# A statically planned attention and two-layer expert kernel: new engine choices for three kinds of operations, and its instruction order searched anew

## The chip, the core and the metric

The program runs on one core of a Trainium2 chip, in one launch. The metric is the device time of that launch in microseconds (us). TensorE (PE in the profile) multiplies matrices, and its weight loads stand beside it as PEld. VectorE (DVE), ScalarE (ACT) and GpSimd (POOL) do elementwise work, and SyncE (SP) issues every transfer.

## The reference, cut to what is computed

```python
# attention: 4 batches, 8 heads, 576 positions, head size 64
scores = q @ k.T / sqrt(64)
x      = log1p(abs(i - j)) / log1p(max(i, 1))        # one number per (i, j)
bias   = relu(x * w1 + b1) @ w2                      # 32 inner units -> 8 heads
attn   = softmax(scores + bias) @ v                  # 2304 tokens x 512
# first expert layer pair, 512 -> 2048 -> 512
g1     = s * relu(attn @ w_in) ** 2 + b
y1     = g1 @ w_out
# second expert layer pair, 512 -> 2048 -> 512
h      = y1 @ w2_in
y2     = (h - tanh(h)) @ w2_out
```

The four large weights come as 64-bit floats, so the kernel also turns them into 32-bit values on VectorE (three instructions for each half of a weight pair, lines 1253, 1256 and 1259). Products are made of two 16-bit parts: each fp32 operand is split into a high and a low half, and three products are added. The second layer pair uses a seven-product block scheme (in_product and out_product) in place of eight.

## The kernel before, in words

The program is one list of tasks. Each task has the engines that could run it with a cost for each (`sc.add({DVE: 0.16, POOL: 0.3}, mx_add, ...)`), the tasks that it depends on, and a priority. Before a single instruction is issued, `Schedule.forward` plays this list through a model in Python: engines become free, transfers land after a planned delay, buffers of a ring come free, and among the tasks that can start first the one with the smallest priority number is taken. The sequence in which the model starts tasks is the order in which each engine's instructions are written into its queue. At run time each engine goes through its own queue in that order and waits on semaphores where an input is late.

Five tables steer the model. `COST` corrects the cost of a kind of task on an engine. `XFER` gives a factor on the length of a transfer and a delay after it. `PORT` says which VectorE tasks count as users of what VectorE and GpSimd share. `ENGINE` limits single tasks to named engines; a key such as `u7.hi` holds for all tasks of that name in its tag. `SHIFT` adds a number to the priority of every key, and it is the result of a search. `QG` is the number of bias row groups whose inner layer may run on GpSimd.

The work in the order of time:

- Weights and bias. The first layer pair's weights are loaded, converted and split. The bias has 36 row groups Q (tags bias0 for Q 0 to 7, up to bias4 for Q 32 to 35); each has four inner-layer instructions (`hid`, lines 727 and 730, one for each quarter of the 32 units' rows), matrix products (`mm`, line 761), and a copy out (`out`).
- Attention. There are 144 units: 128 rows of scores of one head. For each: `qk` (line 1041), bias addition and row minimum of the negated scores on VectorE (`ttr`, line 1073), an offset added to that row value (`mx_add`, line 1081, 128x1 elements), the exponential on ScalarE (`ex`, line 1087, which reads the offset value as its bias), high and low halves (`hi`, `lo_a`, `lo_b`; lines 1097 to 1104), a transposing transfer (`tr`, line 1119), and the product with v (`pv`, line 1132). The tags are u0 to u9 for units 0 to 39 (four units each), u12 for 40 to 47 and u13 to u18 for 16 units each. Four units make a group, which is scaled, split and transposed again (tags x0 to x18).
- First layer pair. Nine blocks of 256 tokens (tags f0 to f8). A block has eight pairs of hidden slices: products into PSUM (`ph`, line 1573), ReLU from PSUM (`relu`, line 1586), square, high and low halves; then 16 product tasks into `po` (line 1645) and the copy out (`out`, lines 1659 and 1664).
- The point called `turn`. When all attention is done, its memory is given to the second layer pair, whose weights are then loaded, converted, split and added up (tags L0, L1, P00 to P11; lines 1253 to 1259, 615 to 618 and 1852).
- Second layer pair. 18 sets (tags I0 to I17 for the first product, J0 to J17 for the second), with seven products each. Here the order of the products on TensorE is fixed in the code, one after the other (`last_pe`). Four products of a set leave PSUM through `copy` on ScalarE (line 2057); the others are read by VectorE. High halves of the result (`split`, key I.lambda) can run on ScalarE or VectorE.

Of the kernel before, what the change touches and what calls it, by code (L numbers as in the profile page):

```python
# [26 lines left out]
SHARE0, QP, QA, SCU, QG = 21, 8, 16, 12, 7  # L27
# [3 lines left out]
AHEAD = 6.97  # L31
# [4 lines left out]
    "u.ttr@dve": 0.84944, "f.hi@dve": 1.152216, "u.hi@dve": 0.87312, "s.in_done@dve": 1.1143, "scan.add@dve":  # L36
    0.8125, "f.lambda@dve": 1.174, "s.out_done@dve": 1.662, "u.lo@pool": 0.9991, "f.lo@pool": 0.782085,
    "bias.lambda@pool": 1.0466, "u.qk@pe": 0.885, "u.pv@pe": 0.97, "u.tr@sp": 1.04, "x.lambda@sp": 1.083,
    "q.fn@sp": 1.36, "J.c@dve": 1.2701, "J.fn@dve": 1.12, "L.lambda@dve": 1.0069, "L.square@act": 0.919,
    "P.wsum@dve": 1.0042, "X.scales@dve": 0.7943, "X.sums@dve": 1.21, "X.xsum@dve": 1.1245, "bias.lambda@dve":  # L40
    1.0453, "bias.out@dve": 1.179, "f.norm@dve": 1.2446, "f.out@dve": 1.0696, "f.scales@dve": 0.4404,
    "k.hi@dve": 1.1296, "k.lambda@dve": 1.047, "q.hi@dve": 1.1098, "s.lambda@dve": 1.0224, "scan.lambda@dve":
    0.857, "v.hi@dve": 1.738, "v.lambda@dve": 1.0251, "w.lambda@dve": 0.993, ".begin@dve": 0.784, ".lambda@dve":
    1.116, "L.scales@dve": 0.961, "L.sums@dve": 0.868, "X.lambda@act": 1.021, "X.lambda@dve": 1.023,
    "q.lambda@dve": 1.026, "w.scale_out@dve": 0.859, "u.lo@act": 0.97, "u.lo_a@act": 0.97, "u.lo_b@act": 0.97,
    "u.lo@dve": 0.97, "u.lo_a@dve": 0.97, "u.lo_b@dve": 0.97, "u.lo_a@pool": 0.97, "u.lo_b@pool": 0.97,
    "f.lo@act": 0.85, "f.lo@dve": 0.85, "f.hi@act": 1.04, "f.hi@pool": 1.04, "u.hi@pool": 0.8, "u.ex@dve": 0.8,
    "u.ex@pool": 0.8, "u.ttr@act": 0.8, "u.ttr@pool": 0.8,
}
XFER = {  # L50
    "bias.fn": (0.79893, 1.75), "f.fn": (1.5147, 1.23), "k.fn": (1.07019, 1.73), "q.fn": (1.05633, 1.81),
    "scan.fn": (0.80982, 2.01), "u.fn": (1.21869, 1.21), "u.tr": (1.0197, 2.23), "v.fn": (0.97218, 2.27),
    "w.fn": (0.91872, 2.03), "x.fn": (1.188, 1.54), "x.lambda": (0.81873, 1.51), "L.fn": (0.87714, 2.6), "J.fn":
    (0.33264, 1.52), "X.fn": (1.54341, 1.41), "o.fn": (0.8514, 0.99), ".fn": (0.78903, 1.4),
}
# [3 lines left out]
    "x.recip": 0.0,  # L59
# [5 lines left out]
    "dve", "u12.lo_a": "pool", "u12.lo_b": "pool", "u13.lo_a": "pool", "u13.lo_b": "pool", "u17.lo_b": "pool",  # L65
# [201 lines left out]
class Schedule:  # L267
# [13 lines left out]
    def add(self, opts, fn, deps=(), prio=0.0, takes=(), uses=(), after=(), share=None):  # L281
# [6 lines left out]
        for e, c in opts.items():  # L288
            if len(opts) == 1 or only is None or e in only:
                if isinstance(c, tuple):  # L290
                    k, d = XFER.get(kind, (0.99, 1.79))
                    t.opts[e] = (c[0] * 0.95 * COST.get(kind + "@" + e, 1.0), c[1] * k, d)
                else:
                    t.opts[e] = c * COST.get(kind + "@" + e, 1.0)
# [2032 lines left out]
```

## Time and profile before

| what | value |
|---|---|
| median of three runs | 1053.27 us (1051.8 to 1054.85) |
| the profiled execution | 1057.96 us |
| its span, first to last instruction | 1056.2 us |
| TensorE busy | 964.1 us, 91% of the span |
| VectorE busy | 881.6 us, 83% |
| ScalarE busy | 667.5 us, 63% |
| GpSimd busy | 250.1 us, 24% |
| mean granted TensorE clock | 0.954 |

The profile is of one execution. It is 4.69 us above the median of the runs, and 1.76 us of it lie outside the span. A share of the whole span says little in this kernel, since the limits differ from stage to stage; the stretches below are therefore read one by one. [...]

### The profile page before, as it was taken

To read this page: it belongs to the slowest core of one execution; us is meant where nothing else is said; L and a number is where in the kernel's file an instruction comes from. 1 tells how busy PE (TensorE), PEld (TensorE's weight loads), DVE (VectorE), ACT (ScalarE), POOL (GpSimd) and SP (SyncE) were. 2 spreads that over 40 slices of the span, in tenths; PEclk is the share of its full clock that TensorE was granted. 3 is DMA by queue.
4 is the path that set the end of the run, shared out by engine and by line. 5 is a ranking of instruction groups with operands and counts; after the bars stand their busy time and mean duration, and the time that the engine had idled before them with its cause. 6 is when DMAs were issued, how large, how long until landed. Compare 5 with 4: busy or idle time off the path is not lost.

```text
span 1056.2 us, 32450 instructions
## 1 busy us (share of the span) xinstructions
PE 964.1 (91%) x13486; PEld 833.2 (79%) x13486; DVE 881.6 (83%) x1918; ACT 667.5 (63%) x1307; POOL 250.1 (24%) x319
## 2 busy tenths in 40 slices
PE   5676678999988999999997999988999999999998
PEld 3233356778767788788886888878999999999998
DVE  6999899876568677786774889999999999999885
ACT  4797659749767565776853687766554555464452
POOL 6146437247542334455511000000000000000000
PEclk9767679899999999999999999998999999999999
DMA  9969995899999879999896904410001100100000
GB/s 341 398 227 216 311 236 119 184 200 252 245 197 230 168 179 176 201 188 207 171 180 104 397 21 138 148 36 12 32 23 32 52 23 22 42 22 23 22 22 22
DMA packets 261444, 153.66 MB, mean 145 GB/s; under 512 B 197680, under 2 KB 229552, under 8 KB 261296
## 3 DMA queue, kind: packets, MB, share of 16 engines
q1 hardware_dynamic: 261296, 151.59, 59.1%
q8 instruction: 105, 1.72, 0.7%
q14 instruction: 43, 0.35, 0.1%
HBM read 84.03 MB, written 20.33 MB: 99 GB/s over the span
## 4 chain that ended last, share of the span: by engine, by line
PE 43%; DVE 9%; ACT 3%; DMA 2%; issue 2%; POOL 1%; SPq 0%; DVEq 0%; ACTq 0%; POOLq 0%
PE acc L2166 14%; PE pa L2038 9%; PE pb L2038 7%; PE po L1645 5%; PE ph L1573 4%; PE po L2166 2%; DMA et<-hl 2%; DVE w2big L1852 2%; DVE w2big L618 1%; PE sp L1041 1%; DVE w1big L618 1%; ACT e L1087 1%; POOL hl L1104 1%; PE xp L1132 1%; DVE hr L1603 1%
## 5 line engine op out<-in xcount | busy, mean ns | idle before, releaser
L1645 PE MATMUL po<-hr,w1big 128*128 128x256 f16 x1728 | 202.9, 274 | 3.6 <-ACT x L1664 2.7
L1104 POOL TENSOR_TENSOR hl<-e,hl 128x64 f16<-128x64 f32 (+1 forms) x200 | 160.2, 818 | 184.9 <-ACT hl L1099 107.2
L1573 PEld LDWEIGHTS <-w1big 128*128 128x128 f16 x1728 | 166.9, 99 | 31.5 <-issue 10.6
L1645 PEld LDWEIGHTS <-w1big 128*128 128x128 f16 x1728 | 165.5, 98 | 26.5 <-issue 7.1
L2038 PEld LDWEIGHTS <-w2big 128*128 128x128 f16 x3024 | 175.2, 99 | 2.2 <-issue 2.1
L2166 PEld LDWEIGHTS <-w1big 128*128 128x128 f16 x3024 | 172.8, 98 | 0.0
L1087 ACT ACTIVATE e<-sp,mx 128x576 f32<-128x576 f32 x144 | 105.6, 735 | 70.3 <-POOL mx L1081 34.3
L1073 DVE CUSTOM_DVE_ANT_0 sp<-sp,bi 128x576 f32<-128x576 f32 x144 | 107.0, 772 | 20.2 <-PE sp L1041 16.2
L1573 PE MATMUL ph<-xt_own,w1big 128*128 128x256 f16 x960 | 113.1, 274 | 3.0 <-ACT r L1586 2.2
L1041 PE MATMUL sp<-ks,qs 64*128 64x288 f16 (+1 forms) x960 | 84.2, 296 | 25.8 <-ACT e L1087 24.8
L1573 PE MATMUL ph<-w1big 128*128 128x256 f16 x768 | 91.2, 276 | 3.3 <-ACT r L1586 2.6
L1041 PEld LDWEIGHTS <-qs 64*128 64x128 f16 (+1 forms) x960 | 48.7, 99 | 53.0 <-issue 42.2
L1132 PEld LDWEIGHTS <-et 128*128 128x128 f16 (+1 forms) x1440 | 54.7, 104 | 41.2 <-issue 21.5
L1132 PE MATMUL xp<-vp,et 128*128 128x64 f16 (+1 forms) x1440 | 65.4, 199 | 19.1 <-DMA et<-hl 11.7
L2166 PE MATMUL acc<-hr,w1big 128*128 128x128 f16 x1296 | 79.9, 219 | 0.0
L1099 ACT ACTIVATE hl<-e 128x576 f16<-128x576 f32 x96 | 64.7, 678 | 23.1 <-DMA et<-hl 20.2
L2166 PE MATMUL acc<-w2big,w1big 128*128 128x128 f16 x1296 | 79.0, 219 | 0.0
L1104 DVE TENSOR_TENSOR hl<-e,hl 128x512 f16<-128x512 f32 (+1 forms) x88 | 48.8, 572 | 15.9 <-ACT hl L1099 13.0
L2038 PE MATMUL pa<-w1big,w2big 128*128 128x128 f16 x960 | 59.9, 219 | 1.7 <-ACT w2big L2057 0.9
L1586 ACT ACTIVATE r<-ph 128x512 f32<-128x512 f32 x72 | 42.3, 590 | 25.8 <-PE ph L1573 21.3
L1591 ACT ACTIVATE r<-r,sq 128x512 f32<-128x512 f32 x72 | 51.2, 718 | 0.9
L2074 ACT ACTIVATE w1big<-w1big 128x512 f32<-128x512 f32 x34 | 21.3, 630 | 45.6 <-DVE w1big L2064 33.4
(229 smaller groups left out, 1757.7 us busy)
## 6 DMA issues: line engine op xcount, KB each, us to landing
bi<-btd SPq DMA_DIRECT2D x64, 288.0 KB, 4.1
w1big<-in_wout SPq DMA_DIRECT2D x12, 1024.0 KB, 6.0
btd<-et SPq DMA_DIRECT2D x36, 295.5 KB, 3.7
w1big<-in_win SPq DMA_DIRECT2D x8, 1024.0 KB, 9.7
w2big<-in_win SPq DMA_DIRECT2D x8, 1024.0 KB, 13.1
x2d<-x SPq DMA_DIRECT2D x36, 128.0 KB, 3.1
w1big<-x2d SPq DMA_DIRECT2D x36, 128.0 KB, 2.3
outT<-xt_own SPq DMA_DIRECT2D x18, 256.0 KB, 2.2
```

The source lines that it names most:

```text
L1041: nc.tensor.matmul(out=out, lhsT=qs.tile[64 * h:64 * h + 64, sq, p * r:p * r + r], rhs=ks.tile[64 * h:64 * h + 64, sk, half * HS:(half + 1 ...
L1073: nc.vector.tensor_tensor_reduce(out=st, in0=st, in1=bi.tile.rearrange("p (a b) -> p a b", a=2), scale=-1.0 / KAP, scalar=3.0e38, op0=ALU. ...
L1087: nc.scalar.activation(out=put(e, row_tile("e")).rearrange("p (a b) -> p a b", a=2), in_=sp.tile[:, :, 0:HS], func=AF.Exp, scale=-1.0, bia ...
L1099: nc.scalar.activation(out=h[:, 0:S], in_=e.tile, func=AF.Copy)
L1104: eng_of(eng).tensor_tensor(out=hl.tile[:, o:o + m], in0=e.tile[:, c:c + m], in1=hl.tile[:, c:c + m], op=ALU.subtract)
L1132: nc.tensor.matmul(out=xp[r0:r0 + r, o:o + 64], lhsT=et.tile[:, n, r0:r0 + r], rhs=vp.tile[:, 0, n % 5, 64 * h:64 * h + 64], start=n == 0, ...
L1573: nc.tensor.matmul(out=ph.tile[:, fi, :], lhsT=win_ap(1, sw, m, f), rhs=xa(sx, m), start=m == 0 and j == 0, stop=m == KM - 1 and j == 2,)
L1586: nc.scalar.activation(out=r.tile, in_=ph.tile, func=AF.Relu)
L1591: nc.scalar.activation(out=r.tile, in_=r.tile, func=AF.Square, scale=sq[:, fp // 4:fp // 4 + 1])
L1645: nc.tensor.matmul(out=po.tile[:, :NB1], lhsT=wout_ap(1, sw, f, c), rhs=rhl[f // 8][:, f % 8, sr, :], start=f == 0 and j == 0, stop=f == K ...
L2038: nc.tensor.matmul(out=bank.tile[:, f * HT:(f + 1) * HT], lhsT=w[:, sw, m, f * 128:(f + 1) * 128], rhs=xs[:, sx, m], start=p in (1, 2, 5) ...
L2166: nc.tensor.matmul(out=bank.tile[:, o + c * HT:o + (c + 1) * HT], lhsT=w[:, sw, f, c * 128:(c + 1) * 128], rhs=g[:, sx, f], start=new and ...
```

## The change

Three operations get a further engine: the offset of the row value may run on ScalarE (`mx_add`, an ACTIVATE with the function Copy and a constant bias), the ReLU of the first layer pair may run on VectorE (a maximum with 0), and the copies of the products of the second pair may run on VectorE. `QG` goes from 7 to 36, so that the inner layer of every bias row group may run on GpSimd, at a planned cost of 5.0e-3 us per column in place of 4.2e-3. The planner's tables are corrected: eight costs of VectorE go up, every transfer's delay goes down by 0.36 us except those of bias rows and of the two transposing transfers, which go up by 0.44 to 0.45 us; `AHEAD` goes from 6.97 to 6.93. GpSimd tasks with a share of 0 no longer wait in the model for VectorE. `ENGINE` has 138 entries in place of 124; of those, 81 are as before. In `SHIFT`, no number is as before (the two sets of numbers have a correlation of 0.59).

In the diff below the entries of the tables are grouped, and only those that the text speaks of are kept.

```diff
-SHARE0, QP, QA, SCU, QG = 21, 8, 16, 12, 7
+SHARE0, QP, QA, SCU, QG = 21, 8, 16, 12, 36
-AHEAD = 6.97
+AHEAD = 6.93
 COST = {
-    "u.hi@dve": 0.87312, "scan.add@dve": 0.8125, "f.lambda@dve": 1.174, "f.scales@dve": 0.4404,
-    "k.hi@dve": 1.1296, "q.hi@dve": 1.1098, "scan.lambda@dve": 0.857, "u.lo_a@dve": 0.97,
-    "bias.lambda@pool": 1.0466,
+    "u.hi@dve": 0.95168, "scan.add@dve": 1.0563, "f.lambda@dve": 1.3736, "f.scales@dve": 0.5065,
+    "k.hi@dve": 1.412, "q.hi@dve": 1.3318, "scan.lambda@dve": 0.9598, "u.lo_a@dve": 1.358,
...
 XFER = {
-    "f.fn": (1.5147, 1.23), "u.fn": (1.21869, 1.21), "u.tr": (1.0197, 2.23), "x.lambda": (0.81873, 1.51),
+    "f.fn": (1.5147, 0.87), "u.fn": (1.21869, 1.65), "u.tr": (1.0197, 2.68), "x.lambda": (0.81873, 1.95),
...
 PORT = {
-    "x.recip": 0.0,
+    "x.recip": 0.0, "x.eps": 0.0,
 ENGINE = {
+    "f0.relu": "act", "f1.relu": "act", "f2.relu": "act", "f3.relu": "act", "f4.relu": "act", "f8.relu": "act",
+    "u18.mx_add": "act+pool", "u15.mx_add": "dve+pool", "u16.mx_add": "dve+pool", "u17.mx_add": "dve+pool",
+    "u9.mx_add": "dve+pool", "u7.mx_add": "pool",
-    "u3.mx_add": "pool",
+    "u3.mx_add": "dve",
+    "bias1.lambda": "act+dve", "bias3.lambda": "act+dve",
-    "u7.hi": "act", "u7.lo_a": "dve", "x2.lo": "dve", "x7.lo": "dve", "x7.hi": "dve", "x17.hi": "dve",
+    "u7.hi": "dve", "u7.lo_a": "pool", "x2.lo": "pool", "x7.lo": "pool", "x7.hi": "act", "x17.hi": "act",
+    "u2.lo_a": "pool", "I7.lambda": "act", "I16.lambda": "act", "I10.lambda": "dve", "I15.lambda": "dve",
-    "I5.lambda": "dve", "I6.lambda": "act",
+    "I5.lambda": "act", "I6.lambda": "dve",
...
+        if only is not None and not any(e in only for e in opts):
+            only = None
...
-                    elif eng == "pool" and t.opts[eng] < self.LONG:
+                    elif eng == "pool" and t.share > 0.0 and t.opts[eng] < self.LONG:
...
             if Q < QG:
-                opts[POOL] = 4.2e-3 * n
+                opts[POOL] = 5.0e-3 * n
...
         def mx_add(eng):
             m = mx["m"]
-            eng_of(eng).tensor_scalar(out=m, in0=m, scalar1=LN_E, scalar2=None, op0=ALU.add)
-        t_mx = sc.add({DVE: 0.16, POOL: 0.3}, mx_add, [t_ttr[u]], d + 1.5)
+            if eng == ACT:
+                nc.scalar.activation(out=m, in_=m, func=AF.Copy, bias=LN_E)
+            else:
+                eng_of(eng).tensor_scalar(out=m, in0=m, scalar1=LN_E, scalar2=None, op0=ALU.add)
+        t_mx = sc.add({DVE: 0.16, POOL: 0.31, ACT: 0.2}, mx_add, [t_ttr[u]], d + 1.5)
...
-            def relu(_, fp=fp, ph=ph, r=r):
+            def relu(e, fp=fp, ph=ph, r=r):
                 put(r, r_p.tile([128, 2, NB1], F32, tag="r", name="r")[:, :, :w])
-                nc.scalar.activation(out=r.tile, in_=ph.tile, func=AF.Relu)
-            tr = sc.add({ACT: 0.21 + 0.8e-3 * 2 * w}, relu, tp + [t_bs], ready - 400, [r], [ph])
+                if e == DVE:
+                    nc.vector.tensor_scalar(out=r.tile, in0=ph.tile, scalar1=0.0, scalar2=None, op0=ALU.max)
+                else:
+                    nc.scalar.activation(out=r.tile, in_=ph.tile, func=AF.Relu)
+            tr = sc.add(
+                {ACT: 0.21 + 0.8e-3 * 2 * w, DVE: 0.12 + 1.05e-3 * 2 * w}, relu, tp + [t_bs], ready - 400, [r], [ph],
+                share=0.0,
+            )
...
         def copy(n, bank):
             i = st[n] = inst("E")
             st["t", n] = sc.add(
-                {ACT: 0.68}, lambda _: nc.scalar.activation(out=home(i), in_=bank.tile, func=AF.Copy, scale=ich),
-                [t] + (first_use["E"] if k < 2 else []), pr - 300, [i], [bank],
+                {ACT: 0.68, DVE: 0.66}, lambda e: copy_scale(home(i), bank.tile, ich, e),
+                [t] + (first_use["E"] if k < 2 else []), pr - 300, [i], [bank], share=0.0,
             )
```

## Rows read from the trace of the kernel before

**Rows 1.** The page: busy us, share of the span and instructions of each engine.
```profile
PE 964.1 (91%) x13486; PEld 833.2 (79%) x13486; DVE 881.6 (83%) x1918; ACT 667.5 (63%) x1307; POOL 250.1 (24%) x319
```

**Rows 2.** Busy time by stretch: stretch, length, each engine, PE clock, DMA share, GB/s.
```profile
0.00:26.00 26.00, 14.12 (x145) 8.32 (x149) 16.27 (x35) 12.62 (x22) 15.66 (x12) 0.95 0.92 340
26.00:106.00 80.00, 53.09 (x459) 25.39 (x451) 78.71 (x155) 66.45 (x134) 33.63 (x27) 0.72 0.87 281
106.00:158.00 52.00, 34.64 (x387) 22.64 (x385) 46.95 (x103) 32.95 (x73) 21.98 (x26) 0.74 1.09 276
158.00:561.00 403.00, 387.15 (x5170) 318.20 (x5166) 300.23 (x801) 283.33 (x633) 177.18 (x253) 0.99 0.96 192
561.00:616.00 55.00, 49.87 (x529) 43.51 (x530) 35.94 (x61) 25.84 (x62) 1.64 (x3) 0.97 0.69 230
616.00:721.00 105.00, 94.17 (x942) 84.18 (x939) 100.20 (x158) 80.66 (x137) 0.00 (x0) 0.99 0.26 82
721.00:845.00 124.00, 123.90 (x2169) 123.91 (x2169) 120.63 (x252) 66.36 (x101) 0.00 (x0) 0.98 0.11 32
845.00:1003.00 158.00, 158.00 (x2828) 158.00 (x2825) 145.03 (x295) 79.49 (x119) 0.00 (x0) 1.00 0.08 26
```

**Rows 3.** TensorE's waits from 158 to 721 us: total, times, longest.
```profile
PE sp L1041 <- ACT e L1087: 8.5, 13, 2.3
PE xp L1132 <- DMA et<-hl: 5.6, 6, 2.5
PE ph L1573 <- ACT r L1586: 4.8, 6, 2.0
PE psum L695 <- DVE w2big L2064: 3.9, 1, 3.9
PE po L1645 <- ACT x L1664: 2.7, 2, 1.6
PE pa L2038 <- ACT w2big L2057: 0.9, 1, 0.9
```

**Rows 4.** The chain that ended last, one piece of it: start, length, what.
```profile
677.92 4.44 DMA w1big<-x2d
```

**Rows 5.** Transfers by line: size or none for transposes, median us to landing.
```profile
et<-hl SPq DMA_TRANSPOSE x144, 4.0
```

**Rows 6.** Waits of all engines from 528 to 561 us.
```profile
ACT e L1087 <- POOL mx L1081: 6.0, 4, 2.3
```

**Rows 7.** Instruction groups of the whole span: busy us, mean ns, idle before.
```profile
L1586 ACT ACTIVATE r<-ph 128x512 f32<-128x512 f32 x72 | 42.3, 590 | 25.8 <-PE ph L1573 21.3 <-DVE hr L1603 4.3
...
L1087 ACT ACTIVATION_READ_ACCUMULATOR e<-sp,mx 128x1 f32 x144 | 28.1, 195 | 0.0
...
L1081 POOL TENSOR_SCALAR mx<-mx 128x1 f32<-128x1 f32 x61 | 18.2, 299 | 42.3 <-DVE mx L1073 36.7 <-DVE nm L1554 2.3 <-DVE s L899 0.5
...
L2064 DVE SCALAR_TENSOR_TENSOR w1big<-pb,cols,w1big 128x512 f32<-128x512 f32 x18 | 13.4, 747 | 8.6 <-PE pb L2038 8.6
...
L1081 DVE TENSOR_SCALAR mx<-mx 128x1 f32<-128x1 f32 x83 | 12.0, 149 | 1.0
```

**Rows 8.** Line 2057, the 72 copies: what ScalarE sat idle for before them.
```profile
  PE pa L2038: 41.8, 35
  PE pb L2038: 9.6, 7
```

**Rows 9.** Groups by shape: inner layer of the bias, weight conversion at two times.
```profile
L730 POOL TENSOR_SCALAR hr<-u_sb,cst_sb 128x512 f32<-128x512 f32 x2 | 4.7, 2342 | 0.2 <-DVE qkc L824 0.2
...
L1259 DVE SCALAR_TENSOR_TENSOR w1big<-w1big 128x1024 uint32<-128x1024 uint32 x16 | 21.5, 1348 | 0.1
...
L1259 DVE SCALAR_TENSOR_TENSOR w2big<-w2big 128x1024 uint32<-128x1024 uint32 x8 | 9.5, 1219 | 0.0
```

**Rows 10.** ScalarE in order of time, one inner-layer instruction of Q = 7: start, length.
```profile
32.66 0.67 ACT L727 ACTIVATE xt_own<-u_sb,cst_sb 128x464 f32<-128x464 f32 x1
```

**Rows 11.** The row values' reads: ns (min/median/max), first and last start.
```profile
L1073 DVE DVE_READ_ACCUMULATOR2_ANT mx<- x144: 132/141/145, 60.6 to 559.4; 128x1 f32 x144
```

More of the change, by code (lines that the diff above doesn't have):

```diff
@@ L35 @@
     "w.square@act": 1.07, "k.hi@act": 1.15, "s.lambda@act": 1.09, "q.hi@act": 1.2, "v.hi@act": 1.14,
[L36 to L48, printed above, removed]
+    "u.ttr@dve": 0.84944, "f.hi@dve": 1.152216, "u.hi@dve": 0.95168, "s.in_done@dve": 1.1143, "scan.add@dve":
@@ new lines @@
+    1.0563, "f.lambda@dve": 1.3736, "s.out_done@dve": 1.662, "u.lo@pool": 0.9991, "f.lo@pool": 0.782085,
+    "u.qk@pe": 0.885, "u.pv@pe": 0.97, "u.tr@sp": 1.04, "x.lambda@sp": 1.083, "q.fn@sp": 1.36, "J.c@dve":
+    1.2701, "J.fn@dve": 1.12, "L.lambda@dve": 1.0069, "L.square@act": 0.919, "P.wsum@dve": 1.0042,
+    "X.scales@dve": 0.7943, "X.sums@dve": 1.21, "X.xsum@dve": 1.1245, "bias.lambda@dve": 1.0453, "bias.out@dve":
+    1.179, "f.norm@dve": 1.2446, "f.out@dve": 1.0696, "f.scales@dve": 0.5065, "k.hi@dve": 1.412, "k.lambda@dve":
@@ new lines @@
+    1.047, "q.hi@dve": 1.3318, "s.lambda@dve": 1.0224, "scan.lambda@dve": 0.9598, "v.hi@dve": 1.738,
+    "v.lambda@dve": 1.0251, "w.lambda@dve": 0.993, ".begin@dve": 0.784, ".lambda@dve": 1.116, "L.scales@dve":
+    0.961, "L.sums@dve": 0.868, "X.lambda@act": 1.021, "X.lambda@dve": 1.023, "q.lambda@dve": 1.026,
+    "w.scale_out@dve": 0.859, "u.lo_a@dve": 1.358, "u.lo@act": 0.97, "u.lo_a@act": 0.97, "u.lo_b@act": 0.97,
+    "u.lo@dve": 0.97, "u.lo_b@dve": 0.97, "u.lo_a@pool": 0.97, "u.lo_b@pool": 0.97, "f.lo@act": 0.85,
@@ L49 @@
+    "f.lo@dve": 0.85, "f.hi@act": 1.04, "f.hi@pool": 1.04, "u.hi@pool": 0.8, "u.ex@dve": 0.8, "u.ex@pool": 0.8,
+    "u.ttr@act": 0.8, "u.ttr@pool": 0.8,
 }
 XFER = {
[L51 to L54, printed above, removed]
+    "bias.fn": (0.79893, 1.39), "f.fn": (1.5147, 0.87), "k.fn": (1.07019, 1.37), "q.fn": (1.05633, 1.45),
@@ L55 @@
+    "scan.fn": (0.80982, 1.65), "u.fn": (1.21869, 1.65), "u.tr": (1.0197, 2.68), "v.fn": (0.97218, 1.91),
+    "w.fn": (0.91872, 1.67), "x.fn": (1.188, 1.18), "x.lambda": (0.81873, 1.95), "L.fn": (0.87714, 2.24),
+    "J.fn": (0.33264, 1.16), "X.fn": (1.54341, 1.05), "o.fn": (0.8514, 0.63), ".fn": (0.78903, 1.04),
 }
@@ L87 @@
 SHIFT = {
-    ".begin": 158.6, ".eye": 204.2, ".fn": -49.3, ".lambda": 60.6, "I0.add": 1197.4, "I0.fn": -551.5,
[120 rows of a table removed]
+    ".begin": -187.5, ".eye": 47.9, ".fn": 197.1, ".lambda": 2487.3, "I0.add": 992.9, "I0.fn": -1197.2,
[121 rows of a table added]
 }
@@ L290, in add @@
                 if isinstance(c, tuple):
-                    k, d = XFER.get(kind, (0.99, 1.79))
+                    k, d = XFER.get(kind, (0.99, 1.43))
                     t.opts[e] = (c[0] * 0.95 * COST.get(kind + "@" + e, 1.0), c[1] * k, d)
@@ L390, in forward @@
             else:
-                if eng == "pool" and cost < self.LONG or eng == "dve" and t.share > 0.0:
+                if t.share > 0.0 and (eng == "pool" and cost < self.LONG or eng == "dve"):
                     port[eng] = at + cost
@@ L1288, in w1_split @@
             sc.add(
-                {ACT: 1.04, DVE: 0.72, POOL: 3.0},
+                {ACT: 1.04, DVE: 0.72, POOL: 3.4},
                 lambda e, j=j: copy_scale(pr[:, 0, j * 1024:(j + 1) * 1024], w32_ap(i, j), c(), e), deps, prio,
```

16 lines of the change are left out of this document (9 added, 7 removed), and 269 rows, old and new, of tables (ENGINE, SHIFT).

## The prediction, made before the changed kernel ran

> **What bounds the kernel now.** I read the first lines of the page first, then busy time by stretch, then TensorE's waits, then the chain that ended last. TensorE is busy for 964.1 of 1056.2 us [rows 1], but that average joins stretches with different limits, and the table by stretch separates them [rows 2].
>
> From 721 us on, TensorE does not stop: 123.90 busy of 124 us, then 158.00 of 158. The order of the products is fixed in the code there, so this tail costs what its products cost, some 330 us to near the end of the span, and no new order of the other engines can shorten it. It can only lengthen it. From 26 to 106 us VectorE is the limit, busy 78.71 of 80, while TensorE has gaps and its granted clock is 0.72 of full speed. From 158 to 561 us TensorE is the limit again, with 403 - 387.15 = 15.9 us idle. From 561 to 616 it is idle 5.1 us and from 616 to 721 another 10.8; in the last of these VectorE is busy 100.20 of 105, so there the weight preparation of the second layer pair on VectorE sets when the tail begins.
>
> What a better order can win is therefore part of 15.9 + 5.1 + 10.8 = 31.8 us between 158 and 721. Named waits make up most of it [rows 3]: 8.5 us for the exponential that frees the scores' PSUM, 5.6 for transposes, 4.8 for the ReLU, and 3.9 + 2.7 + 0.9 around the start of the second layer pair. Idle time of 0 to 158 us (158 - 14.12 - 53.09 - 34.64 = 56.2 us) is not counted, because VectorE and the weight transfers set that stretch. The chain shows what one ill-timed transfer costs late: 4.44 us for a load of tokens at 678 us [rows 4].
>
> **The change, part by part.** The limits in the engine table take back much of what the words of the change give, so I count what is really opened.
>
> (a) Corrected delays. Counted from the end of its issue, the planner's old figure for a transpose is 1.2 + 1.4 x 1.0197 + 2.23 - 1.24 = 3.6 us; the new one is 4.1. The median to landing in the trace is 4.0 [rows 5], if it counts from there, so the correction points the right way, and the order should ask for transposed tiles later. Bounds: nothing, and all of the 5.6 us that TensorE waited for them after 158 us [rows 3]. I take -1.5, a quarter: a tile that is asked for later needs other work in between, and not every place has it.
>
> (b) The offset on ScalarE. Each tag from u0 to u18 now has an entry for this operation, and only u18 (units 128 to 143) names ScalarE: 16 of 144 instructions, the last before the attention ends. There the exponential waited 6.0 us in four waits for the offset on GpSimd [rows 6]. An offset takes 149 ns on VectorE and 299 on GpSimd; the nearest small ScalarE instruction, the read of the accumulator, takes 195 [rows 7]. On ScalarE it stands directly ahead of the exponential that needs it, which drops one crossing between engines; what is queued behind it is the next exponential, and the transposes wait for that. Bounds: -6.0 if all four waits were on the path, +3.1 if 16 x 0.195 us of ScalarE time lie on it. TensorE was not idle for most of those waits, so I take -1.0.
>
> (c) ReLU on VectorE. Blocks 0 to 4 and 8 are held on ScalarE; blocks 5, 6 and 7 are free, 24 of 72. On ScalarE one takes 590 ns. No row shows this operation on VectorE; the nearest, a 512-column instruction that reads PSUM, takes 747 [rows 7], while the planner counts 658. VectorE is free for 25% of 158 to 561 us [rows 2], and that free time hides them; if it does not, the unplanned part is 24 x 0.09 = +2.1. The most to win is the 4.8 us that TensorE waited for the ReLU [rows 3]. I take -0.5, since VectorE is the slower engine for it. [...] The rows side with ScalarE for data in PSUM.
>
> (d) Copies on VectorE. 72 copies of the second layer pair may move, with no entry that limits them. TensorE is saturated there, so the gain is 0, at best the 0.9 us of one wait ahead of 721 [rows 3]. For the other side: ScalarE sat waiting for the product ahead of 35 + 7 = 42 copies [rows 8], so at 30 of 72 it was still busy, and the planner gives a copy to whichever engine is free first. A set has 14 products of 24 matmuls, so the 2169 matmuls from 721 to 845 us [rows 2] are 6.5 sets with 26 copies, of which 42% is 11. At 0.747 us [rows 7] they add 8.2 us to VectorE, which has 124 - 120.63 = 3.4 us free there [rows 2]: 4.8 us too much. After 845 us it has 13 us free. The planner knows VectorE's load and will avoid most of this, and work of splitting moves the other way, so I take 0 and keep +4.8 as the bad end. [...]
>
> (e) Inner layer on GpSimd. bias1 to bias4 are limited to ScalarE and VectorE, and bias0 up to Q = 6 had GpSimd already. New are the four instructions of Q = 7. They ran on ScalarE at 0.67 us each [rows 10]; one of about that width takes 2342 ns on GpSimd [rows 9]. Freed at best: 4 x 0.67 = 2.7 us of ScalarE, which is not the limit there. On the other side, 10.4 us more of GpSimd (with a margin for its slower instances) can slow VectorE: the same conversion instruction takes 1348 ns in the first 160 us, where GpSimd works, and 1219 after 616 us, where it does nothing [rows 2, 9]. 129 of 1348 ns over 10.4 us is +1.0. I take 0. The first scores wait for these rows; ScalarE had them at 33.3 us, GpSimd would have them some 10 us later, and the first row value is read at 60.6 us [rows 10, 11], which covers it. Without that cover, the full 10 us would stand at the start.
>
> (f) The order itself and the other 57 new or changed engine entries. They trade single instructions of 0.15 to 0.7 us between engines, in both directions (u7.hi to VectorE; u7.lo_a, x2.lo, x7.lo off it). The waits ahead of 721 us that (a) to (c) leave are 3.9 + 2.7 + 0.9 = 7.5 us [rows 3]: the good end. The bad end is one more late load in front of the weight preparation, 4.4 us [rows 4]. I take -2.0, about a quarter again: the search starts from a model that has been corrected, but it worked on the model, not on the chip.
>
> Sum: -1.5 - 1.0 - 0.5 + 0 + 0 - 2.0 = -5.0 us. On the profiled execution that is 1057.96 - 5.0 = 1053.0; that execution stands 4.69 above the median of the runs, so the prediction against the median is 1053.27 - 5.0 = 1048.3 us.
>
> **Rivals.** A measurement of this kernel can tell about 0.3%, or 3.2 us.
>
> A, the waits move and nothing is gained: 1053.3 us. For it: only 16, 24 and 4 instructions of three of the four parts are really opened, the tail is out of reach, and both orders come from a search on the same kind of model. Against it: the model's delays now fit the trace better.
>
> B, slower through VectorE in the second layer pair: (d) at its bad end, decided once more than 3.4 / 0.747, that is some four or five, extra copies fall to VectorE between 721 and 845 us. Then TensorE, never idle there, would wait for the halves that VectorE makes: 1053.3 + 4.8 = 1058.1 us. For it: VectorE is busy 97% there and the copies have a smaller priority number than the rest of its work. Against it: the planner sees most of it.
>
> C, slower through a late load or a late instruction of VectorE between 616 and 721 us: 1053.3 + 4.4 = 1057.7 us. For it: the chain runs through VectorE there, and every transfer delay in the plan has become shorter, by 0.36 us, for loads like the one of 4.44 us. Against it: the loads were the smaller part of the waits.
>
> **How the numbers follow.** The forecast has a chance of 0.55, A 0.25, B 0.12, C 0.08. So faster than 1050.1 us is 0.55, within 0.3% is 0.25, slower than 1056.4 us is 0.20. For the range the bounds of the six terms are taken as independent: below the taken values they reach 4.1, 5.0, 4.3, 0.9, 2.7 and 5.5 us, together (root of the sum of squares) 10 us, so 1038; above them 1.5, 4.1, 2.6, 4.8, 1.0 and 6.4, together 9.5 us, so 1058. That takes in A and C and ends at B.
>
> **What would show it.** Right: TensorE's idle time from 158 us to the start of its unbroken tail falls from 31.8 to about 27 us, and the tail begins near 716 us on this execution's scale; the waits for transposes shrink; the offsets of the last units stand on ScalarE and its waits for GpSimd there are gone; few of the 72 copies stand on VectorE, and TensorE shows no wait after the tail has begun. Wrong: waits for copies, halves or gates in the tail (B); a longer stretch between the end of attention and the tail with VectorE waiting for transfers (C); or the same idle time with other names (A). The time of the front, up to the first block's products, should hardly move; if it falls by several us, the order at the front was worth more than I count, and (f) is mis-sized.

## The result, and the profile after

The changed kernel is slower. Its median is 1065.2 us (four runs, 1062.47 to 1066.33) against 1054.06 for the kernel before (four runs as well); the ratio is 1.0104, with a 95% interval of 1.0078 to 1.0131. That is +11.0 us, with 8.2 and 13.8 as bounds. The forecast was 1048.3, so it has the wrong sign, and the result lies outside its range. All differences below are ratios of this kind times 1054 us, each against runs of the kernel before that were timed beside it. Where an expectation quotes an earlier run (-0.9 us for the offsets, 10.1 for all choices), that is the plain difference of two medians.

The two profiled executions differ by less than the medians, 1062.47 to 1057.96 us: the first is the fastest of its kernel's runs and the second stands above its median. The trace shows where time went, and the timed runs how much.

The page's first line and busy time by stretch for the kernel after, in the stretches of [rows 2]; its lines are 7 to 16 numbers higher than before.

```profile
PE 958.9 (90%) x13486; PEld 830.7 (78%) x13486; DVE 886.4 (84%) x1889; ACT 661.4 (62%) x1306; POOL 272.2 (26%) x349
```

```profile
0.00:26.00 26.00, 12.76 (x141) 7.20 (x144) 15.82 (x34) 12.88 (x21) 16.29 (x11) 0.95 0.92 340
26.00:106.00 80.00, 50.77 (x463) 26.00 (x457) 79.03 (x155) 66.02 (x133) 37.50 (x27) 0.70 0.91 284
106.00:158.00 52.00, 27.66 (x312) 18.07 (x311) 43.52 (x97) 32.72 (x69) 19.78 (x19) 0.69 1.12 247
158.00:561.00 403.00, 387.89 (x5127) 318.17 (x5126) 297.08 (x762) 283.90 (x641) 194.66 (x288) 0.99 0.96 194
561.00:616.00 55.00, 51.67 (x626) 44.54 (x621) 37.56 (x59) 28.57 (x71) 3.98 (x7) 1.00 0.77 241
616.00:721.00 105.00, 97.18 (x955) 86.22 (x953) 98.19 (x159) 79.03 (x139) 0.00 (x0) 0.98 0.25 82
721.00:845.00 124.00, 119.31 (x2100) 119.01 (x2098) 121.76 (x252) 62.90 (x95) 0.00 (x0) 0.99 0.10 30
845.00:1003.00 158.00, 158.00 (x2827) 157.95 (x2825) 151.39 (x308) 74.11 (x112) 0.00 (x0) 1.00 0.09 27
```

Against [rows 2], TensorE's idle time from 0 to 158 us grew from 56.2 to 158 - 12.76 - 50.77 - 27.66 = 66.8 us, 7.0 of these 10.6 between 106 and 158. From 158 to 561 it went only from 15.9 to 15.1. The 4.6 us that are missing from 721 to 845 are mostly the tail's later start, as the next rows show: scores and the second pair's second product (line 2182) of the kernel after, then the same two of the kernel before; each line gives the first and the last start.

```profile
L1048 PE MATMUL sp<-ks,qs x960: 279/283/445, 38.5 to 561.2; 64*128 64x288 f16 x154, 64*64 64x288 f16 x38
...
L2182 PE MATMUL acc<-hr,w1big x1296: 216/219/220, 730.4 to 1045.8; 128*128 128x128 f16 x186
L2182 PE MATMUL acc<-w2big,w1big x1296: 217/219/220, 749.1 to 1055.1; 128*128 128x128 f16 x186
```

```profile
L1041 PE MATMUL sp<-ks,qs x960: 279/283/444, 37.5 to 557.5; 64*128 64x288 f16 x154, 64*64 64x288 f16 x38
...
L2166 PE MATMUL acc<-hr,w1big x1296: 217/219/314, 726.2 to 1041.3; 128*128 128x128 f16 x186
L2166 PE MATMUL acc<-w2big,w1big x1296: 217/219/219, 745.2 to 1050.6; 128*128 128x128 f16 x186
```

The last scores come 3.7 us later, the tail begins 4.2 us later (730.4 against 726.2), and it lasts 1055.1 - 730.4 = 324.7 us against 324.4. The tail itself is unchanged. The first product of the first expert block (into `ph`), after and before:

```profile
L1583 PE MATMUL ph<-xt_own,w1big x960: 269/273/421, 162.7 to 681.0; 128*128 128x256 f16 x192
L1573 PE MATMUL ph<-xt_own,w1big x960: 269/273/421, 153.5 to 678.2; 128*128 128x256 f16 x192
```

It comes 9.2 us later. Most of that is planned: `Schedule.forward` puts this product at 158.6 us in the kernel after and at 149.5 in the kernel before (planned times, worked out from the two kernels' own planners). From there to the last scores the kernel after takes 398.5 us and the kernel before 404.0, so a good part of the late start is made up. Other traces agree: the five that keep the old order and its bias engines up to the last scores have 152.6 to 154.1 us for the first product and 402.2 to 404.7 from there, the two that keep the new order 162.8 and 164.7, and 396.7 and 399.9. The span grew by 4.5 us only, since TensorE's idle time from 158 us to its unbroken tail went from 31.8 to 30.7 us, and the same 13486 matmuls took 5.2 us less (958.9 busy against 964.1).

TensorE's waits of the kernel after, from 0 to 158 us, and then from 158 to 721 us, which answers to [rows 3]:

```profile
PE xp L1142 <- DMA et<-hl: 18.7, 8, 5.2
PE sp L1048 <- ACT e L1097: 16.8, 9, 3.7
PE gram L875 <- DMA w1big<-in_kT: 12.1, 3, 6.9
PE pb L768 <- ACT et L622: 5.7, 3, 3.2
```

```profile
PE sp L1048 <- ACT e L1097: 10.0, 18, 1.2
PE ph L1583 <- ACT r L1599: 2.4, 2, 1.4
PE po L1661 <- ACT x L1680: 2.4, 4, 1.1
PE xp L1142 <- DMA et<-hl: 2.1, 3, 1.0
```

The first line is the largest change. Before, the same wait from 0 to 158 us was 6.1 us in five waits:

```profile
PE xp L1132 <- DMA et<-hl: 6.1, 5, 1.9
```

After 158 us it fell from 5.6 [rows 3] to 2.1, and the ReLU's from 4.8 to 2.4, but the wait for the exponential rose from 8.5 to 10.0.

The choices as the kernel after uses them (groups of the whole span, answering to [rows 7]; idle time at the end):

```profile
L1599 ACT ACTIVATE r<-ph 128x512 f32<-128x512 f32 x67 | 39.4, 588 | 21.0 <-PE ph L1583 18.4 <-DVE hr L1619 2.2
...
L2080 DVE SCALAR_TENSOR_TENSOR w1big<-pb,cols,w1big 128x512 f32<-128x512 f32 x18 | 13.4, 745 | 3.5 <-PE pb L2054 3.5
...
L618 DVE TENSOR_SCALAR w1big<-pa,cols 128x512 f32<-128x512 f32 x9 | 6.7, 742 | 0.0
...
L618 DVE TENSOR_SCALAR w2big<-pb,cols 128x512 f32<-128x512 f32 x5 | 3.7, 742 | 0.0
L1597 DVE TENSOR_SCALAR r<-ph 128x512 f32<-128x512 f32 x5 | 3.4, 679 | 0.0
L618 DVE TENSOR_SCALAR w2big<-pa,cols 128x512 f32<-128x512 f32 x4 | 3.0, 741 | 0.0
L1089 ACT ACTIVATE mx<-mx 128x1 f32<-128x1 f32 x8 | 1.6, 198 | 4.2 <-DVE mx L1080 4.2
```

So 18 copies and 5 ReLUs run on VectorE and 8 offsets on ScalarE; three inner-layer pieces of the bias went from ScalarE to GpSimd. These 34 instructions are the opened choices. In all, 303 of 4180 tasks changed their engine.

### The profile page after: what moved, and what is told of

The parts are those of the page before. It is cut to its first block, busy times and chain, and to the rows that moved or that the text cites. A ratio compares the mean times of both kernels' runs of the same rounds, so it can differ in the third digit from the quotient of the medians.

```text
span 1060.7 us, 32489 instructions
## 1 busy us (share of the span) xinstructions
PE 958.9 (90%) x13486; PEld 830.7 (78%) x13486; DVE 886.4 (84%) x1889; ACT 661.4 (62%) x1306; POOL 272.2 (26%) x349
## 4 chain that ended last, share of the span: by engine, by line
PE 40%; DVE 11%; DMA 3%; issue 3%; ACT 2%; SPq 1%; POOL 1%; POOLq 0%; DVEq 0%; ACTq 0%
PE acc L2182 13%; PE pa L2054 8%; PE pb L2054 6%; PE ph L1583 5%; PE po L1661 5%; PE po L2182 2%; DMA et<-hl 2%; DVE w2big L625 1%; PE sp L1048 1%; DVE w2big L1266 1%; DVE w2big L1868 1%; DVE w2big L1269 1%; DVE hr L1619 1%; DVE w1big L625 1%; PE xp L1142 1%
## 5 line engine op out<-in xcount | busy, mean ns | idle before, releaser
L1114 POOL TENSOR_TENSOR hl<-e,hl 128x64 f16<-128x64 f32 (+1 forms) x209 | 167.4, 815 | 147.0 <-ACT hl L1109 70.9
L1583 PEld LDWEIGHTS <-w1big 128*128 128x128 f16 x1728 | 164.6, 98 | 28.9 <-issue 10.6
L1080 DVE CUSTOM_DVE_ANT_0 sp<-sp,bi 128x576 f32<-128x576 f32 x144 | 107.1, 772 | 17.8 <-PE sp L1048 11.4
L1109 ACT ACTIVATE hl<-e 128x576 f16<-128x576 f32 x87 | 58.7, 677 | 22.3 <-DMA et<-hl 16.9
L1114 DVE TENSOR_TENSOR hl<-e,hl 128x512 f16<-128x512 f32 (+1 forms) x79 | 54.6, 695 | 19.2 <-ACT hl L1109 16.2
L1599 ACT ACTIVATE r<-ph 128x512 f32<-128x512 f32 x67 | 39.4, 588 | 21.0 <-PE ph L1583 18.4
## 6 DMA issues: line engine op xcount, KB each, us to landing
w1big<-in_win SPq DMA_DIRECT2D x8, 1024.0 KB, 10.2
```

Source lines behind the costliest of these rows:

```text
L1080: nc.vector.tensor_tensor_reduce(out=st, in0=st, in1=bi.tile.rearrange("p (a b) -> p a b", a=2), scale=-1.0 / KAP, scalar=3.0e38, op0=ALU. ...
L1109: nc.scalar.activation(out=h[:, 0:S], in_=e.tile, func=AF.Copy)
L1114: eng_of(eng).tensor_tensor(out=hl.tile[:, o:o + m], in0=e.tile[:, c:c + m], in1=hl.tile[:, c:c + m], op=ALU.subtract)
L1583: nc.tensor.matmul(out=ph.tile[:, fi, :], lhsT=win_ap(1, sw, m, f), rhs=xa(sx, m), start=m == 0 and j == 0, stop=m == KM - 1 and j == 2,)
L1599: nc.scalar.activation(out=r.tile, in_=ph.tile, func=AF.Relu)
```

## The experiments

Most of the kernels below replace the planner by a fixed list: the order of the tasks and the engine of each. The old list gives the kernel before, instruction by instruction, and the new list the kernel after. Such a list can be cut, joined and edited one entry at a time. The lines of these kernels stand 227 numbers higher than those of the kernel after.

```diff
     def run(self):
-        self.forward(True)
+        for n, e in zip(ORDER.split(), ENG):
+            self.tasks[int(n)].fn(NAMES[e])
```

### The new order, swapped in by stretches

The first matmul of the first expert block and `turn` are the two joints. That matmul is the sum that the block's scale needs. The first product into `ph` follows it directly in the old list, but 48 tasks later in the new one (planned at 147.5 and 158.6 us), so the front ends a little earlier than the first expectation says.

```diff
-old list
+seg_new_front:  new list up to the first expert matmul, then old
+seg_new_middle: old list up to the first expert matmul, new up to turn, then old
+seg_new_tail:   old list up to turn, then new
+seg_old_tail:   new list up to turn, then old
```

> The order and the engines of the changed kernel up to the first product of the first layer pair (the first matmul into ph), then those of the kernel before. Theory F (the loss is made in the front, where the changed kernel starts its first block 9 us later): slower than before by 5 to 11 us. Theory L (the loss is made after the attention has ended, by the copies on VectorE): within 2 us of before. Theory M (the loss is made between): within 2 us of before.

> The order of the kernel before up to the first product of the first layer pair, then that of the changed kernel up to the end of attention, then that of before. Theory M: slower by 5 to 11 us. Theories F and L: within 2 us of before.

> The order of the kernel before up to the end of attention, then that of the changed kernel, with its 18 copies on VectorE. Theory L: slower by 5 to 11 us, with waits of TensorE after the second layer pair has begun. Theories F and M: within 2 us of before.

> The order of the changed kernel up to the end of attention, then that of the kernel before. Theories F and M: slower than before by 8 to 11 us, as the changed kernel is. Theory L: within 3 us of before. If the stretches add up, this one's difference and that of the kernel with only the tail changed together make the 11 us of the whole change.

Measured: the front +11.4 us (7.2 to 15.6), the middle +8.6 (5.8 to 11.6), the tail +4.0 (2.2 to 5.8), front and middle together +6.3 (3.3 to 9.4). The last two add up to 10.3, nearly the whole 11.0. Front and middle cost more one by one than together, so joints between two orders cost time themselves, and those two numbers can't be read as the price of a stretch. No swapped stretch measured faster than the old one. In the trace of the swapped tail the second product runs from 728.3 to 1052.6 us, 324.3 us, so the 18 copies cost nothing there and the waits that Theory L named are missing; what its trace lost lies ahead of 728 us, between the last scores and that product (171.0 us against 168.7 in the kernel before).

### The choices alone, in the old order

```diff
 old order, engines of:
-8 offsets of u18: dve x4, pool x4
+8 offsets of u18: act
-5 ReLUs (f5, f6, f7 x3): act
+5 ReLUs (f5, f6, f7 x3): dve
-18 copies of I: act
+18 copies of I: dve
-3 inner-layer pieces of bias0: act
+3 inner-layer pieces of bias0: pool
```

All four pairs together are the first run, the ReLUs alone the second, copies alone the third, offsets alone the fourth, and the bias pieces alone the fifth.

> The kernel before with its own instruction order, replayed as a fixed list, and only the newly opened choices set as the changed kernel uses them: 8 row-maximum offsets on ScalarE, 5 ReLUs and 18 accumulator copies on VectorE, 3 inner-layer pieces of the bias on GpSimd. 34 instructions of 4180 change their engine, none its place. Theory 1 (the loss is the new order, the choices cost only what they add to VectorE between the end of attention and the tail): +1 to +3 us, of it 2.0 from the three ReLUs (680 ns each) that stand after the change to the experts' second stage, the copies nothing. Theory 2 (the choices carry the loss, the order is harmless): +8 to +11 us. If the choices gain in an order that was not searched for them: below -1 us.

> The kernel before, its order unchanged, with 5 ReLUs moved from ScalarE to VectorE, the three of the last block but one among them. Theory 1 (between 561 and 721 us VectorE is the bound, so a ReLU there costs its whole 680 ns): +2 us, with the first scaled copy out of PSUM at the tail's start some 2 us later. Rival (VectorE has free time there that takes them, as the prediction said): 0 +- 1 us. Rival 2 (ScalarE's 590 ns each come off a chain): below -1 us.

> The kernel before, its order unchanged, with the 18 accumulator copies that the changed kernel gives to VectorE moved there from ScalarE, and nothing else. All four choices together cost 10 us in this order and the ReLUs alone 1.6. Theory (the tail is where VectorE has no room: 18 copies of 742 ns are 13.4 us more on an engine that was busy 36 to 39 of each 40 us, so some accumulators are read late and TensorE stands idle): +5 to +8 us, nearly all of it between 780 and 950 us, where TensorE is no longer busy 40 of 40 us. Rival (the copies fit into VectorE's pauses, as the prediction said, and offsets or bias pieces carry the rest): 0 to +1 us.

> The kernel before, its order unchanged, with the row-maximum offset of 8 of the 16 softmaxes of the last attention unit moved from VectorE or GpSimd to ScalarE (202 ns each in the changed kernel). Theory (these sit near the end of the attention, where ScalarE's exponentials wait for them; an in-line offset takes away a hand-over between engines): -1 to 0 us. Rival (ScalarE's 202 ns stand on the chain from scores to exponentials): +1 to +3 us, which would be the part of the loss of all choices together that copies and ReLUs leave over.

> The kernel before, its order unchanged, with three inner-layer pieces of the bias's first block moved from ScalarE to GpSimd. If the choices' costs add up (10.1 together, less 6.0, 1.6 and -0.9), +3 us, because a piece takes several times longer on GpSimd and the bias row behind it comes later in the front. If these pieces have slack, 0 +- 1 us, and the choices' costs do not simply add.

Measured: together +10.2 us (7.4 to 13.1); ReLUs +1.6 (-0.1 to 3.3); copies +6.0 (4.1 to 7.9); offsets -1.6 (-3.3 to +0.2); bias pieces +5.3 (3.5 to 7.2). The four add up to 11.3, so within their intervals they explain the sum. The first of my theories, that the choices cost little beyond three ReLUs, fell here: in the old order they cost about as much as the whole change.

The copies, in the old order. TensorE's busy time in the tail with the copies alone, in slices of 40 us (columns as in [rows 2]), and its waits from 727 us to the end:

```profile
780.00:820.00 40.00, 39.81 (x711) 39.67 (x709) 39.41 (x87) 13.09 (x21) 0.00 (x0) 1.00 0.07 22
820.00:860.00 40.00, 37.89 (x675) 37.62 (x673) 39.40 (x90) 17.73 (x27) 0.00 (x0) 1.00 0.11 36
860.00:900.00 40.00, 40.00 (x717) 39.94 (x715) 38.53 (x77) 19.85 (x31) 0.00 (x0) 1.00 0.10 32
900.00:940.00 40.00, 38.42 (x684) 38.18 (x682) 37.17 (x78) 20.88 (x32) 0.00 (x0) 1.00 0.13 39
```

```profile
PE psum L929 <- DVE cols L2139: 2.2, 3, 1.6
PE pa L2281 <- DVE w1big L845: 1.6, 1, 1.6
```

TensorE, busy for 40.00 of 40 us in each of these slices before, now waits for VectorE. The second product runs from 721.5 to 1050.6 us, 329.1 us against 324.4: the tail is 4.7 us longer. In the kernel after, the same 18 copies do not do this. There VectorE is even busier, 121.76 + 151.39 = 273.2 us from 721 to 1003 against 271.5 here, and from 727 us on TensorE waits once, for 0.2 us, and in the swapped tail not at all. So it is the place of the copies in VectorE's queue that matters.

The bias pieces. GpSimd and TensorE in order of time in the run of the bias pieces alone (start, length, what, idle before); GpSimd has nine pieces there, six of them as before:

```profile
17.02 12.85 POOL L964 TENSOR_SCALAR hr<-u_sb,cst_sb 128x512 f32<-128x512 f32 x4 [0.25 <-PE pb L995]
29.86 1.94 POOL L964 TENSOR_SCALAR xt_own<-u_sb,cst_sb 128x496 f32<-128x496 f32 x1
31.77 6.61 POOL L964 TENSOR_SCALAR hr<-u_sb,cst_sb 128x480 f32<-128x480 f32 x3
```

```profile
26.13 1.87 PE L995 MATMUL pb<-hr,cst_sb 128*32 128x496 f32 x4 [1.41 <-POOL hr L964]
29.93 1.86 PE L995 MATMUL pb<-hr,cst_sb 128*32 128x496 f32 x2 [1.94 <-POOL hr L964]
...
38.44 0.58 PE L995 MATMUL pb<-hr,cst_sb 128*32 128x464 f32 x2 [0.78 <-POOL hr L964]
```

Four pieces in a row take 12.85 us, TensorE waits for GpSimd three times, and the first scores start at 41.8 us where they started at 37.5. In the kernel after they start at 38.5, so the new order had put most of this right.

The ReLUs. Three of the five stand between 616 and 721 us. VectorE's group there in the run of the ReLUs alone, and the stretch (length, VectorE, PE clock, DMA share, GB/s):

```profile
L1824 DVE TENSOR_SCALAR r<-ph 128x512 f32<-128x512 f32 x3 | 2.0, 682 | 0.0
```

```profile
616.00:721.00 105.00, 101.34 (x158) 0.99 0.26 83
```

VectorE has no pause ahead of them and is the limit in that stretch [rows 2], so I take the 2.0 us to count in full. That is argued: the run's interval agrees with 2.0 but does not exclude 0.

### Order and engines taken apart

```diff
-old order, old engines
+engines_old_order_engines_new: old order, all 303 engines as in the new list
-new order, new engines
+choices_closed_in_new: new order, the 34 opened instructions on their old engines
```

> The kernel before in its own order, with all 303 instructions that the changed kernel puts on another engine moved there, each in its old place of the order. Theory 1 (the order itself carries the loss; the engine choices of the new plan carry little): +1 to +4 us. Theory 2 (the engine choices carry it): +8 to +12 us. An order and its engines were chosen together, so a list that fits neither may cost more than both: above +12 us would say only that the two can't be parted in this way.

> The changed kernel in its own new order, with the newly opened choices taken back: the 8 offsets as in the old plan, the 5 ReLUs and 18 copies on ScalarE, the 3 bias pieces on ScalarE. Theory 1 (the new order was searched around the choices and hides the copies in its tail, but not the ReLUs): 2 us below the changed kernel, about +9 us on the kernel before. Theory 2 (the choices cost in this order as they do in the old one): 8 to 10 us below the changed kernel, +1 to +3 us on the kernel before. Rival (the new order needs them, because ScalarE's queue fills up without them): above the changed kernel, +12 us or more.

Measured: old order with all new engines +28.8 us (25.7 to 31.9), which says only that order and engines can't be parted as wholes. New order with the choices taken back: +8.6 (5.9 to 11.3), 2.4 us less than with them. That is theory 1 of that run: in its own order the choices cost some 2 us, which the two intervals do not tell from 0, and the other 8.6 us are there without a single opened choice in use. So is TensorE's wait for transposes in the front: 18.4 us up to 165 us, with the choices 18.7.

### The planner's corrected delays alone

```diff
-COST, XFER, PORT, AHEAD of before
+COST, XFER, PORT, AHEAD of after
 SHIFT, ENGINE, QG and all engine options of before
```

> The kernel before with only the corrected delays of the planner (the factors of the costs, the transfer table, the lead of 6.93 instead of 6.97 us) and its own priority shifts and engine entries; none of the three kinds of operations gets a new choice. Theory 1 (the priorities and the delays are one fit: with other delays the planner lays another order that no search has improved): +5 to +25 us. Theory 2, the prediction's step (better delays give a better order by themselves): -5.6 to 0 us.

Measured: +33.4 us (30.5 to 36.4). Correcting the tables without a new search lays a much worse order (the costs that stand in the code are as before). If the search of the kernel after began there, which is not on record, it won back about two thirds of this, and not all.

The planner can also be asked what it thinks of the orders, since either kernel's planner can play a fixed list. These are planned ends of the last task, and no run stands behind them. The order above ends at 1061.2 us by its own planner. The corrected planner has the new list at 1042.7 us and the old one at 1041.0, so it sees 1.7 of the 11.0 us. The new order with the choices taken back, which both planners can price, stands 2.9 us behind the old one by the corrected planner and 15.3 by the planner of before, where 8.6 were measured. Neither is right, and the one that goes with the new order flatters it.

### The queue in the front

Two edits of the new list in which no engine's own order changes, only SyncE's queue. In the first, some bias rows stand up to seven places later than in the old sequence, because the work that makes them comes later in the new list.

```diff
 new list, SyncE's queue up to the first expert matmul:
-103 transfers as in the new list
+front_queue_old: 103 transfers in the old list's sequence
 new list, six 1 MB weight loads planned from 93 to 128 us:
-as in the new list
+new_loads_later: each behind the next two transposes
```

> The changed kernel with one edit: the transfers that SyncE issues up to the first expert matmul (103 of them) go out in the old kernel's sequence, in the same places of the order; no compute instruction moves. Theory 1 (in the front the transposes and bias rows stand behind weight and bias loads that the new order issues sooner, and PE waits for them): PE's waits for transposed probabilities before 165 us fall from 18.7 us towards 6.1 us, the first expert matmul comes 3 to 9 us sooner, and the whole is 2 to 6 us below the changed kernel, that is +5 to +9 us on the kernel before. Rival (the queue's order is not the cause; the late start is the compute order of the bias and attention): within 1.5 us of the changed kernel, some +10 us on the kernel before, with the first expert matmul still at about 162 us.

> The changed kernel with six loads of second-stage weights (1 MB each, issued between 93 and 128 us of the plan) each moved behind the next two transposes in SyncE's queue; no engine's own order changes. Theory (in the front the transposes of the probabilities wait behind these loads, 5.2 to 7.7 us for two or three issues, and TensorE waits for them, 18.7 us before 165 us against 6.1): these waits fall below 13 us and the whole gains 2 to 5 us on the changed kernel, that is +6 to +9 us on the kernel before. Rival (the loads are needed where they stand: the conversions of the weights wait instead and the experts begin later): slower than the changed kernel, above +12 us on the kernel before. Rival 2 (the transposes are slow for other reasons): within 1.5 us of the changed kernel.

Measured: +22.8 us (19.0 to 26.7) and +22.7 (19.8 to 25.4) on the kernel before, some 12 us worse than the kernel after. With the old sequence TensorE's wait for transposes up to 165 us did not fall but rose, from 18.7 to 25.9 us. SyncE's longest wait there was for bias rows that were not made yet; the same wait of the kernel after stands below it:

```profile
SPq L702 <- ACT et L849: 52.5, 13, 10.7
SPq L475 <- ACT et L622: 13.8, 7, 2.7
```

Both rows are idle time of the queue itself, 52.5 us in 13 waits against 13.8 us in seven: what stands behind such a wait goes out after it. With the loads moved back, TensorE's waits from 0 to 165 us read:

```profile
PE sp L1275 <- ACT e L1324: 26.7, 12, 9.6
PE gram L1102 <- DMA w1big<-in_kT: 12.2, 2, 7.4
PE pc L1548 <- DVE w1big L1496: 12.2, 3, 9.7
PE xp L1369 <- DMA et<-hl: 7.2, 3, 4.6
```

The wait for transposes did fall, from 18.7 to 7.2 us, so loads ahead of them are a part of it. But converted weights and exponentials came late instead, up to 9.7 us in one wait, and the whole got slower. That is the first rival of this run: the loads are needed where they stand.

### Where the new front loses

```diff
+seg_new_first80:   new list up to 80 us of the plan, then old
+first80_bias_act:  the same, the three bias pieces on ScalarE
+first120_bias_act: new list up to 120 us, then old, the pieces on ScalarE
 old list:
+offset16_in_old:   all 16 offsets of u18 on ScalarE
```

> The new order up to the matmul planned at 80 us, and the old order and engines from there to the end. Theory 1 (the new front loses before 80 us: the weights of one expert are converted first, the bias rows later, and TensorE is busy 5.7 us less in 0 to 80 us than before): +4 to +8 us. Theory 2 (the loss comes between 80 and 165 us, where TensorE waits for the transposes): 0 to +2 us. The swap at the first expert matmul cost +10 us, joint included.

> The new order up to the matmul planned at 80 us, then the old order and engines, with the three bias pieces back on ScalarE. Theory 1 (the pieces on GpSimd cost in any order what they cost in the old one, 3 to 5 us, by the first scores coming 4 us later, and the rest of the new front's first 80 us gains): -2 to -4 us on the kernel before, a version that beats both. Theory 2 (the new order had room for them): +1 to +2 us, as with the pieces on GpSimd.

> The new order up to the matmul planned at 120 us, then the old order and engines, with the three bias pieces back on ScalarE. If the new front loses between 80 and 120 us: +4 us or more. If it loses only between 120 and 165 us, where its longest waits for transposes stand: within 2 us of the swap at 80 us with the same pieces. The swap at the first expert matmul, with the pieces on GpSimd, cost +10 us.

> The kernel before, its order unchanged, with all 16 row-maximum offsets of the last attention unit on ScalarE. If taking away the hand-over to GpSimd or VectorE is what counts: -1 to -3 us, below the run with 8 of them. If ScalarE's own time stands on the chain: 0 to +2 us. The run with 8 stood at -0.9 us with an interval that holds zero, so anything within 1.5 us leaves it at no measurable change.

Measured: up to 80 us +1.4 us (-0.9 to 3.7), and with the pieces back +0.8 (-1.6 to 3.3), so in the new order the pieces cost nothing that can be told. Up to 120 us +3.6 (1.4 to 5.8), up to the first expert matmul +11.4. Up to 80 us no loss can be told, up to the first expert matmul it is clear. Up to 120 us the interval overlaps those at 80, so where between 80 us and that matmul the loss begins is not settled, and each of these numbers holds the price of its joint. All 16 offsets on ScalarE: +0.7 (-0.9 to 2.4), no measurable change. No version was measurably faster than the kernel before; the lowest was the old order with 8 offsets on ScalarE.

## Why the prediction was wrong, step by step

The step that failed is (f), the order. It was put at -2.0 us, with one late load, +4.4, as its bad end; the new order without any opened choice measured +8.6 (the corrected delays of (a) are in that order too). I reasoned that a search on a corrected model starts from better ground. The runs showed two other things: the priorities are fitted to one set of delays, so that new delays alone cost 33 us, and the order that the search then found does not get back to where the old one stood.

The place was excluded as well. The prediction set aside the idle time of 0 to 158 us, "because VectorE and the weight transfers set that stretch", and looked for the gain and all rivals behind it. What sets a stretch can get worse: TensorE lost 10.6 us there, the first expert product came at 162.7 us in place of 153.5, and the swaps put a loss between 80 us and the first expert matmul. That the front carries the 8.6 us is likely and not shown: the late product was planned, part of it was made up by the last scores, and the swap includes a joint whose own price is not known. What in the new order delays the transposes there is open in part. Loads ahead of them count, but both edits of the queue made the whole worse.

(a) came out in kind and in place, though no run shows that the corrected delays did it: after 158 us the wait for transposes fell by 3.5 us of 5.6. It was given back there as 1.5 us more wait for exponentials, and it rose by 12.6 us in the front, which the step did not look at.

(b) can't be told from nothing. It was forecast at -1.0 for up to 16 offsets; only 8 moved, and alone they measured -1.6 with zero just inside the interval, while all 16 measured +0.7. The offset takes 198 ns on ScalarE, near the 195 of the row that bounded it [rows 7]. The four waits for GpSimd [rows 6] are gone, but from 528 to 561 us ScalarE now waits as often for the row value itself:

```profile
ACT mx L1089 <- DVE mx L1080: 4.2, 4, 1.9
```

(c) was mis-sized: -0.5 forecast; +1.6 measured alone (-0.1 to 3.3), with 5 of 24 moved. The 679 ns per ReLU lie inside the bounds, but the cover did not hold. I hid all of them in VectorE's free time of 158 to 561 us; three of the five stand after 616, where VectorE is the limit. This ReLU reads 32-bit values from PSUM, and ScalarE was the faster engine for it in the kernel after: 588 ns, against 679 on VectorE.

(d) read the table wrongly, and its 0 came out partly by luck. A copy's key is I.lambda, so the entries for I6, I10 and I15 do pin copies to VectorE: 12 of the 18 that went there, where I counted on few. In the old order they made the tail 4.7 us longer (and the kernel 6.0 slower), which is the mechanism of rival B (VectorE out of room in the tail) at about its price of 4.8. In the new order the tail stayed at 324.7 us, so rival B did not decide this case. The price by the row, 747 ns, was the right one: 741 to 742 were measured. The planner's price for a copy on VectorE, 0.66 us, is too low here.

(e) was wrong in its cover. I let the first row value at 60.6 us hide a late bias row; the trace shows the first scores themselves 4.3 us later, and the run +5.3 us, in the old order. The +1.0 that went into the range left out what the step itself names for a start without that cover. In the new order nothing of it can be told.

Rival A's time did not come, but behind 158 us its picture did: almost the same idle time, 30.7 us for 31.8, under other names, where the prediction asked for about 27. Rival C did not come: the time from the last row value to the tail grew by about 1 us only (562.4 to 730.4, against 559.4 to 726.2), and the chain's wait for tokens, 4.44 us in [rows 4], is 2.36 there. A fourth rival was missing: the new order is simply worse.

## What to carry to other kernels

An order found by search belongs to the model that it was searched in: change the model's delays, and the search has to win back what the change of model cost before it can gain anything. An order can look better in the model that it was found with than it is: here that model saw 1.7 of 11.0 us. Before an idle stretch is set aside as "bound by something else", ask what it would cost if that something came later. A choice of engine is priced by the place that it gets in a queue: 18 copies of 742 ns cost nothing that shows in one order and 6 us in another.

## What the runs showed of the hardware

The second input of VectorE's accumulating read of PSUM showed no price of its own in the kernel after: 741 to 742 ns for the scaled copy (line 618, one operand besides the scalars), 741 to 745 with an addend from SBUF (line 2080). The ReLU, which compares the same 512 columns with a constant and reads no scale, took 679 (line 1597).

The granted clock had short falls that differed between the traces of nearly the same instructions. Busy time of TensorE and granted clock in stretches of 2 us for the kernel before, around 580 us:

```profile
578.00:580.00 2.00, 0.54 (x5) 0.45 (x5) 1.58 (x6) 1.16 (x2) 0.00 (x0) 0.96 0.27 82
580.00:582.00 2.00, 2.00 (x11) 1.44 (x10) 1.66 (x4) 1.37 (x3) 0.00 (x0) 0.50 0.56 119
582.00:584.00 2.00, 2.00 (x15) 1.54 (x14) 0.58 (x1) 0.06 (x1) 0.00 (x0) 0.69 0.96 389
584.00:586.00 2.00, 2.00 (x21) 1.80 (x19) 0.64 (x2) 1.26 (x2) 0.00 (x0) 1.00 1.03 422
```

TensorE had been busy for 0.54 of 2 us; in the next two stretches the granted clock was 0.50 and 0.69, and from 584 us on 1.00 again. In the swap at 80 us, where the old order's instructions follow as well, it was busy for 0.29 of the 2 us from 572 on, and the clock stayed at 1.00 there and in the rows behind:

```profile
572.00:574.00 2.00, 0.29 (x3) 0.11 (x2) 1.67 (x6) 0.31 (x1) 0.00 (x0) 1.00 0.15 31
```

By the rows of 0.50 and 0.69, with 11 and 15 matmuls where the row behind them has 21, such a fall is worth 1 to 2 us (an estimate), so one trace beside another can't settle differences of that size; the timed runs have to.
